# An mLSTM cell and a quick-GELU block on one core: another order in the second chunk

## The chip, the cores and the metric

The kernel runs on one core of a Trainium2 chip. The metric is the device time of one execution in microseconds (us), from six runs. One more execution was taken with the hardware profiler; its trace is what "the profile" means below. The engines are TensorE (PE, with its weight loads PEld), VectorE (DVE), ScalarE (ACT), GpSimd (POOL) and SyncE (SP), which issues most DMAs.

## The reference

An mLSTM cell runs over 768 steps for 4 batches of 8 heads (head dimension 40); its output is reshaped to 3072 tokens of 320 values and goes through a two-layer block with a quick GELU.

```python
for t in range(S):
    m_new = np.maximum(f_gate[:, :, t] + m, i_gate[:, :, t])
    f_stab = np.exp(f_gate[:, :, t] + m - m_new)
    i_stab = np.exp(i_gate[:, :, t] - m_new)
    m = m_new
    C = f_stab * C + i_stab * np.einsum('bhd,bhe->bhde', vt, kt)
    n = f_stab * n + i_stab * kt
    h_tilde = np.einsum('bhde,bhe->bhd', C, qt)
    denom = np.maximum(np.abs(np.einsum('bhd,bhd->bh', n, qt)), 1.0)
    y[:, :, t] = sigmoid(o_gate[:, :, t]) * h_tilde / denom

h = x @ w_in                      # 3072 x 320 @ 320 x 2048
out = (h * sigmoid(1.702 * h)) @ w_out   # 2048 x 320
```

## The kernel before

**Chunks.** The 768 steps are cut into six chunks of 128 (`w` = 0 to 5). Within a chunk the recurrence is written as attention: scores of queries and keys, times decay weights, times values, plus the queries times the state carried from the chunk before. "The second chunk" is `w = 1`, called chunk 1 here. `b` is one of the four batches.

**The main loop.** For each chunk `w` the kernel computes the up products (GELU hidden values of the chunk's 512 tokens), then the down products. The attention of chunk `w + 1` is put between the down blocks of chunk `w`. The order on every engine is the order in which the code issues the work: it is written out by hand, and each engine runs its queue in that order and waits where an input is not there.

**Chunk 0 is special.** Its up and down products are plain (`up`, `down`); from chunk 1 on they use sums of blocks that save products (`up_fast`, `down_fast`). The weights `w_in` and `w_out` come in as raw bits in twenty pieces; `fetch(n)` loads one, `convert(n)` turns it into 32-bit floats in two ACT and four DVE instructions. Pieces 10 to 19 are `w_out`; they are still being loaded and converted beside the down blocks of chunk 0.

**The 16 down blocks of chunk 0** (`blocks`, L796) go in the order: two blocks for each b, then one for each b, then one for each b. Block `i` = 12 to 15 ends the sum of batch `i - 12`: DVE copies it from PSUM to `o_sb` (L568) and ACT's queue stores it (L569). After the blocks whose numbers are in `stops` (L797) the next list of `attention(1)` (L645 to L649) is run. So the lists after blocks 10, 12 and 15 are: the first two seams; values of b = 2, 3 and the scalings; the last two seams, the new states and the carry.

**The parts of attention that matter here:**
- `values(w, ...)`: PE products of weights and values (`p_o`, L363) and of queries and state (`p_i`, L368). Then for each b a chain of seven DVE instructions (L383 to L393) makes `y`, reading the o gates `eo` in L391, and GpSimd copies 64 of its columns (L395).
- `scale_values` (L409) and `scale_state` (L415): GpSimd multiplies the values `v_st` and the `state` of one b in place by decay factors. They have to come after the products that read the old contents.
- `seam(w, b)`: three PE transposes of `y` (L402), the third of which needs the columns that GpSimd copied; ACT copies the result to `xT` (L403), the input of the up products.
- `new_states`: PE products of keys and scaled values (`p_c`, L428). `carry`: DVE adds them to the scaled state (L436); GpSimd sets the ones column of `v_st` (L439).
- `gates_out`: ACT's tanh of the o gates, in place (L343). It stands after the eight exponentials of `weights(1, 2)` (L335).

**The sums of `w_out`** (`weight_sums`, L583): sums 0 and 1 make `t1` and `t2` for the fast down products of chunk 1, which come some 35 us later. They need `w_out` converted in full.

**SP's queue.** All loads go through it in order. In the loop over chunk 0's up products, at `j == 4` (L776 to L781), come the o gates of chunk 1 (640 KB, one DMA), then piece 17 (two DMAs), then the values of chunk 1 (640 KB, one DMA of the same shape); pieces 18 and 19 and the keys follow. At block 10 the queue gets 32 small loads of chunk 2's keys and queries (`load_blocks(2)`, L117), which DVE transposes (L302) at the start of chunk 1's up products. The core's DMAs, loads and stores, share eight completion counters in turn, and a DMA is not issued before the one ahead of it on the same counter is complete.

Of the kernel before, what the change touches and what calls it, by code (L numbers as in the profile page):

```python
# [34 lines left out]
def kernel(  # L35
# [120 lines left out]
    def fetch(n):  # L156
        if 6 <= n < 10:
            bits[n] = gp.tile([128, 512, 2], U32, tag="g", name="bits")
        else:
            room = xs if n == 19 else big[:, n if n < 6 else (n - 10) % 6, :]  # L160
            bits[n] = room.bitcast(U32).rearrange("p (a two) -> p a two", two=2)
        for r, c, src in pieces[n][1]:
            dst = bits[n][r, c].rearrange("p a two -> p (a two)")
            if len(src.shape) == 3:
                dst = dst.rearrange("p (j m) -> p j m", j=src.shape[1])
            nc.sync.dma_start(out=dst, in_=src)
# [188 lines left out]
    def values(w, *bs, states=False):  # L355
        po, pi = {}, {}
        for b in bs:
            po[b] = ps_a.tile([L, H, D1], FP, tag="a", name="p_o")
            for p in range(NP):
                for i in range(2):  # L360
                    h = 2 * p + i
                    for t in HALVES:
                        T.matmul(po[b][t, h, :], wt[w, b][:, p, i, t], v_st[:, b * H + h, :], start=True, stop=True)  # L363
        for b in bs if w else ():
            pi[b] = ps_a.tile([L, H, D1], FP, tag="a", name="p_i")
            for p in range(NP):
                for t in HALVES:
                    T.matmul(pi[b][t, 2 * p:2 * p + 2, :].rearrange("p a b -> p (a b)"), qT[w, b][:, p, t],  # L368
                             state[:, b * NP + p].rearrange("p a b -> p (a b)"), start=True, stop=True)
        if states:  # L370
            for b in bs:
                scale_values(w, b)
        if states and w:

            new_states(w)
            for b in bs:
                scale_state(w, b)
        for b in bs:
            u = po[b]
            if w:  # L380
                u = work.tile([L, H, D1], FP, tag="u", name="u")
                g = cols[w][:, BH + b * H:BH + (b + 1) * H].unsqueeze(2).to_broadcast([L, H, D1])
                V.tensor_tensor(out=u, in0=pi[b], in1=g, op=OP.mult)  # L383
                V.tensor_tensor(out=u, in0=po[b], in1=u, op=OP.add)

            den = work.tile([L, H, 1], FP, tag="den", name="den")
            V.tensor_scalar(out=den, in0=u[:, :, D:D1], scalar1=-1.0, scalar2=1.0, op0=OP.mult, op1=OP.max)
            V.tensor_tensor(out=den, in0=u[:, :, D:D1], in1=den, op=OP.max)
            V.reciprocal(out=den, in_=den)
            z = eo[w][:, b * H:(b + 1) * H, :]  # L390
            V.scalar_tensor_tensor(out=z, in0=z, scalar=1.0, in1=u[:, :, 0:D], op0=OP.add, op1=OP.mult)  # L391
            y = ys[w, b] = work.tile([L, DM + 64], FP, tag="y", name="y")
            V.scalar_tensor_tensor(out=y[:, 0:DM].rearrange("p (h d) -> p h d", d=D), in0=z, scalar=0.5,  # L393
                                   in1=den.to_broadcast([L, H, D]), op0=OP.mult, op1=OP.mult)
            G.tensor_copy(out=y[:, DM:DM + 64], in_=y[:, DM - 64:DM])  # L395
# [185 lines left out]
    def weight_sums(n):  # L581
        out_, in0, in1 = ((t1, w01, w00), (t2, w11, t1), (t4, w10, t2), (w01, w11, w01))[n]
        V.tensor_tensor(out=out_, in0=in0, in1=in1, op=OP.subtract)  # L583
# [51 lines left out]
    def attention(w):  # L635
        if w > 1:

            return [[(columns, w)], [(weights, w, 0), (weights, w, 1)],
                    [(scores, w, 0), (hidden_sums, w - 1, 1, range(4), 3), (scores, w, 1), (weights, w, 2),
                     (weights, w, 3)],  # L640
                    [(values, w, 0), (values, w, 1), (scores, w, 2), (scores, w, 3)] +
                    [(scale, w, b) for b in (0, 1) if w + 1 < NW],
                    [(seam, w, 0), (seam, w, 1), (last_values, w)], [(carry, w)] if w + 1 < NW else [],
                    [(seam, w, 2)], [(seam, w, 3)]]
        return [[(columns, w)], [(weights, w, 0), (weights, w, 1)], [(scores, w, 0), (scores, w, 1)],  # L645
                [(weights, w, 2), (gates_out, w), (values, w, 0, 1), (scale, w, 0), (scale, w, 1)],
                [(weights, w, 3), (scores, w, 2), (scores, w, 3)], [(seam, w, 0), (seam, w, 1)],
                [(values, w, 2, 3), (scale, w, 2), (scale, w, 3)],
                [(seam, w, 2), (seam, w, 3), (new_states, w), (carry, w)]]  # L649

    def last_values(w):
        values(w, 2, 3, states=w + 1 < NW)
# [1 line left out]
    def run(calls):  # L654
        for f, *args in calls:
            f(*args)
# [98 lines left out]
    for w in range(NW):  # L755
        more = w + 1 < NW
        for j in range(NF // 2):
            if w == 0 and j == 0:
                for pair_ in range(2):
                    for i, g in enumerate(hidden_of(0, pair_)):  # L760
                        A.activation(out=g, in_=first[pair_][i], func=AF.Gelu_apprx_sigmoid)
                    if pair_ == 0:
                        weights_in(0)
            elif w == 0 and j % 2 == 0:
                weights_in(j // 2)
                up(j, j == 2)
            elif w and j % 4 == 0:
                up_fast(w, j, next_keys if more and j == 0 else None)
            if w == 0 and j == 0:
                load_blocks(1, 0)  # L770
                spread(1)
                load_blocks(1, 1)
            if w == 1 and j == 3:
                weight_sums(3)
            if more:
                if j == (0 if w else 4):  # L776
                    load(w + 1, "o")
                if j == 4:
                    if w == 0:
                        fetch(17)  # L780
                    load(w + 1, "v")  # L781
                    if w:
                        spread(w + 1)
                if j == (4 if w else 6):
                    load(w + 1, "k")
                if w and j == 3:
                    for b in range(2, 4):
                        transposes(w + 1, b)
            if w and j in (3, 7):
                hidden_sums(w, 0, (j // 4 * 2, j // 4 * 2 + 1), 1, 2)  # L790
                if j == 3:
                    hidden_sums(w, 0, (0, 1), 3, 4)
        side = attention(w + 1) if more else []
        if w == 0:

            blocks = [(lambda b=b, n=n: down(w, b, n)) for ns in ((0, 1), (2,), (3,)) for b in range(B) for n in ns]  # L796
            stops = (0, 1, 5, 6, 8, 10, 12, 15)  # L797
        else:
            blocks = down_fast(w, 0) + down_fast(w, 1)
            stops = (0, 1, 2, 4, 8, 10, 11, 12)  # L800
        for i, block in enumerate(blocks):
            if w == 0:
                weights_in(4 + i)
                if i == 0:
                    load_gates(2)
                if i == 2:
                    for b in range(B):
                        transposes(1, b, slice(0, 1))
                    first_sums((0, 1))
                    for b in range(B):  # L810
                        transposes(1, b, slice(1, 2))
                if i == 10:
                    load_blocks(2)
            elif w + 2 < NW and i == 0:
                load_gates(w + 2)
                load_blocks(w + 2)
            block()
            if i in stops and side:
                run(side.pop(0))
            if w == 1 and i == 1:  # L820
                weight_sums(2)
            if w:
                for at, c, *what in ((0, 0, (2, 3), 3), (1, 0, (2, 3), 4), (1, 1, range(4), 1),
                                     (5, 1, range(2), 2), (6, 1, range(2, 4), 2), (7, 1, range(4), 4)):
                    if i == at:
                        hidden_sums(w, c, *what)
                if i == 2 and not more:
                    hidden_sums(w, 1, range(4), 3)
            elif i in (12, 14):
                weight_sums(i // 2 - 6)  # L830


# [28 lines left out]
```

## Time and profile before

| | |
|---|---|
| six runs, median (lowest to highest) | 490.01 us (487.5 to 492.44) |
| the profiled execution, its own time | 490.47 us |
| its span in the trace | 488.8 us |
| granted TensorE clock | 1.0 of full speed |
| PE busy | 478.0 us (98%), 4076 instructions |
| PE weight loads busy | 395.8 us (81%) |
| DVE / ACT / POOL busy | 342.1 / 221.0 / 63.9 us |
| DMA | 44.87 MB, mean 92 GB/s, nearly all on SP's queue |

Times in a trace are counted from the span's start. PE's busy time is modelled from pipelined matmuls, so two that follow each other overlap a little in the list. A line of the timeline has the start, the length, the engine, the code line, the operation, the tiles written and read, the shape, how many instructions are merged into it and, in square brackets, how long the engine was idle before it and what released it. In the stage before 62 us the kernel loads and converts `w_in` and runs chunk 0's attention; from 66 to 115 us it runs the down blocks of chunk 0 with chunk 1's attention between them; from 119 us the up products of chunk 1 follow, and from there on the chunks repeat.

### The profile page before, as it was taken

The numbers are of one execution on the slowest core, as the hardware profiler recorded it, in microseconds if no ns is written. First come the engines' busy times: TensorE is split into PE (matmuls) and PEld (weight loads), VectorE is DVE, ScalarE is ACT, GpSimd is POOL, SyncE is SP. The second block draws the span as 40 slices with busy tenths as digits, with TensorE's granted clock in tenths as the row PEclk, the third lists the DMA queues.
The fourth block names the chain that finished last, engine by engine and source line by source line (L and its number), as shares of the span: only waits on it lengthen the run. The fifth ranks groups of instructions, "written<-read, shape, count | busy, mean of one in ns | idle before, by whom it ended". The sixth has DMA issues, their size and how long they took to land. (4 is left out here: it accounts for less than half of the span.)

```text
span 488.8 us, 10443 instructions
## 1 busy us (share of the span) xinstructions
PE 478.0 (98%) x4076; PEld 395.8 (81%) x4076; DVE 342.1 (70%) x855; ACT 221.0 (45%) x575; POOL 63.9 (13%) x103
## 2 busy tenths in 40 slices
PE   7999998999999999999999999999999999999997
PEld 4874455777788999777999877999977999977897
DVE  8788878659978965677776586686666786254831
ACT  6757764501468500476800474900364930255300
POOL 4030001314000240000322000232000120000000
PEclk9999999999999999999999999999999999999999
DMA  9999779964896200996100696300293000000000
GB/s 127 180 258 320 118 189 200 156 77 70 113 237 70 31 28 15 142 229 74 17 29 1 108 256 77 35 28 3 65 264 34 1 1 30 28 1 0 1 27 28
DMA packets 175953, 44.87 MB, mean 92 GB/s; under 512 B 164352, under 2 KB 169504, under 8 KB 175904
## 3 DMA queue, kind: packets, MB, share of 16 engines
q1 hardware_dynamic: 175328, 43.55, 48.4%
q8 instruction: 32, 0.52, 0.5%
q10 hardware_dynamic: 576, 0.66, 0.4%
q14 instruction: 17, 0.14, 0.1%
HBM read 40.17 MB, written 4.01 MB: 90 GB/s over the span
## 5 line engine op out<-in xcount | busy, mean ns | idle before, releaser
L613 PE MATMUL p_out<-w_out_sb,g 128*128 128x160 f32 x480 | 69.8, 301 | 0.0
L403 ACT COPY xT<-p_x 128x384 f32<-128x384 f32 x24 | 10.8, 481 | 128.1 <-PE p_x L402 112.0
L613 PEld LDWEIGHTS p_out<-w_out_sb,g 128*128 128x128 f32 x480 | 66.3, 190 | 0.9
L524 DVE TENSOR_TENSOR g<-p_u,g 128x256 f32<-128x256 f32 x80 | 33.7, 424 | 44.7 <-PE p_u L516 35.0
L521 ACT COPY g<-p_u 128x256 f32<-128x256 f32 x120 | 43.1, 377 | 41.3 <-PE p_u L516 37.1
L528 ACT ACTIVATE g<-g 128x256 f32<-128x256 f32 x120 | 42.4, 425 | 39.1 <-DVE g L524 39.1
L337 POOL TENSOR_SCALAR_AFFINE_SELECT wt<-wt 128x1024 f32<-128x1024 f32 x20 | 22.7, 1136 | 238.5 <-ACT wt L335 208.7
L618 DVE TENSOR_TENSOR o_sb<-o_sb,p_out 128x160 f32<-128x160 f32 x70 | 21.4, 317 | 42.2 <-PE p_out L613 41.8
L335 ACT ACTIVATE wt<-wt,cols 128x128 f32<-128x128 f32 x160 | 47.9, 393 | 0.0
L516 PE MATMUL p_u<-xT,w_in_sb 128*128 128x256 f32 x160 | 38.9, 382 | 0.0
L516 PE MATMUL p_u<-xs,big 128*128 128x256 f32 x160 | 37.9, 379 | 0.0
L544 PE MATMUL p_v<-xT,w_in_x 64*128 64x512 f32 x80 | 37.0, 602 | 0.0
L544 PE MATMUL p_u<-xT,w_in_x 64*128 64x512 f32 x80 | 37.0, 602 | 0.0
L353 DVE TENSOR_TENSOR wt<-p_s,wt 128x512 f32<-128x512 f32 x48 | 30.4, 682 | 8.8 <-POOL wt L337 6.7
L564 PE MATMUL p_out<-w_out_sb,g 128*128 128x320 f32 x128 | 36.1, 436 | 0.0
L613 PE MATMUL p_out<-t,big 128*128 128x160 f32 x240 | 35.5, 301 | 0.0
L516 PEld LDWEIGHTS p_u<-xT,w_in_sb 128*128 128x128 f32 x160 | 29.6, 190 | 5.4 <-DVE o_sb L618 1.5
L516 PEld LDWEIGHTS p_u<-xs,big 128*128 128x128 f32 x160 | 30.0, 190 | 4.6 <-ACT g L521 0.2
L613 PEld LDWEIGHTS p_out<-t,big 128*128 128x128 f32 x240 | 33.3, 190 | 0.2
L564 PEld LDWEIGHTS p_out<-w_out_sb,g 128*128 128x128 f32 x128 | 23.8, 190 | 9.9 <-issue 0.5
L524 DVE TENSOR_TENSOR g<-p_v,g 128x256 f32<-128x256 f32 x80 | 29.8, 415 | 0.0
L363 PEld LDWEIGHTS p_o<-v_st,wt 128*64 128x64 f32 x768 | 23.9, 138 | 5.7 <-DVE w_out_sb L237 3.3
(168 smaller groups left out, 851.5 us busy)
## 6 DMA issues: line engine op xcount, KB each, us to landing
wt<-m_row SPq DMA_DIRECT2D x20, 512.0 KB, 7.0
eo<-in_o_gate_dram SPq DMA_DIRECT2D x5, 640.0 KB, 5.6
v_st<-in_v_dram SPq DMA_DIRECT2D x5, 640.0 KB, 8.9
k_st<-in_k_dram SPq DMA_DIRECT2D x5, 640.0 KB, 11.4
out_dram<-o_sb SPq DMA_DIRECT2D x20, 160.0 KB, 1.8
big<-in_moe_w_in_dram SPq DMA_DIRECT2D x5, 512.0 KB, 6.7
k_bl<-in_k_dram SPq DMA_DIRECT2D x40, 64.0 KB, 2.9
q_bl<-in_q_dram SPq DMA_DIRECT2D x40, 64.0 KB, 2.8
```

The lines of the kernel that those rows point to most:

```text
L335: A.activation(out=x[:, h, :], in_=x[:, h, :], func=AF.Exp, scale=-1.0, bias=cols[w][:, b * H + h:b * H + h + 1])
L337: G.affine_select(out=x, in_=x, compare_op=OP.is_ge, fill=0.0, base=0, pattern=[[0, H], [1, L]], channel_multiplier=-1)
L353: V.tensor_tensor(out=wt[w, b][:, :, i, :], in0=pw[i], in1=wt[w, b][:, :, i, :], op=OP.mult)
L363: T.matmul(po[b][t, h, :], wt[w, b][:, p, i, t], v_st[:, b * H + h, :], start=True, stop=True)
L516: T.matmul(p[k][:, ts[t]], a[:, k // 2, k % 2 * 128:(k % 2 + 1) * 128], b, start=first, stop=True, skip_group_check=True)
L521: A.copy(out=g[k][i][:, ts[t]], in_=chain[k][:, ts[0]])
L524: V.tensor_tensor(out=g[k][i][:, ts[t]], in0=p[k][:, ts[pt]], in1=g[k][i][:, ts[t]], op=OP.add)
L528: A.activation(out=dst, in_=dst if src is None else src, func=AF.Gelu_apprx_sigmoid)
L544: T.matmul(p[k], w_in_x[r, k, :], x[r, 2, :], start=False, stop=True, skip_group_check=True)
L564: T.matmul(po, gs[w, f // 2][:, f % 2, b * L:(b + 1) * L], w_out_sb[:, f, :], start=(f == 0), stop=(f == NF - 1))
L613: T.matmul(po, a(f), b[:, f, :], start=(f == 0), stop=(f == NH - 1))
L618: V.tensor_tensor(out=dst, in0=x, in1=po, op=OP.add)
```

## The change

Four edits, all around chunk 1's attention:

- SP's queue: the values of chunk 1 are loaded where the o gates were, and the o gates after piece 17, where the values were.
- Values of b = 2, 3: GpSimd scales `v_st` and `state` before DVE's chains and GpSimd's copies of `y` are issued, not after them. The new states stay where they were, after block 15; `values` is reached through `last_values` with `states=True`, and a new branch for `w == 1` scales the state alone.
- The last two seams are run after block 14 and the new states and carry after block 15, so `stops` has nine entries and `attention(1)` nine lists.
- Weight sums 0 and 1 are both issued after block 11, ahead of DVE's copy of block 12, instead of after blocks 12 and 14.

```diff
         if states:
             for b in bs:
                 scale_values(w, b)
-        if states and w:
+        if states and w == 1:
+            for b in bs:
+                scale_state(w, b)
+        elif states and w:
 
             new_states(w)
             for b in bs:
...
-                [(values, w, 2, 3), (scale, w, 2), (scale, w, 3)],
-                [(seam, w, 2), (seam, w, 3), (new_states, w), (carry, w)]]
+                [(last_values, w)], [(seam, w, 2), (seam, w, 3)], [(new_states, w), (carry, w)]]
 
     def last_values(w):
         values(w, 2, 3, states=w + 1 < NW)
...
-                if j == (0 if w else 4):
+                if w and j == 0:
                     load(w + 1, "o")
                 if j == 4:
-                    if w == 0:
-                        fetch(17)
                     load(w + 1, "v")
                     if w:
                         spread(w + 1)
+                    else:
+                        fetch(17)
+                        load(1, "o")
...
-            stops = (0, 1, 5, 6, 8, 10, 12, 15)
+            stops = (0, 1, 5, 6, 8, 10, 12, 14, 15)
...
-            elif i in (12, 14):
-                weight_sums(i // 2 - 6)
+            elif i == 11:
+                weight_sums(0)
+                weight_sums(1)
```

On the engines' queues this moves: on PE the six transposes L402 ahead of the last four-step down block; on DVE two L583 ahead of the copy of block 12; on ACT the last store behind the two copies L403; on POOL two L409 and two L415 ahead of two copies L395; on SP the two 640 KB loads past the two DMAs of piece 17. No instruction is added or removed.

## The prediction

> **What bounds the kernel now.** I read the busy time by stage first, to see where TensorE (PE) is not busy; then PE's waits, to learn what ends its idle time; then the engines in order of time around the two waits.
>
> Busy time by stage (start:end, length, then busy us and instructions of each engine, clock, DMA share, GB/s):
>
> ```profile
> core 0: us, PE busy (x) PEld busy (x) DVE busy (x) ACT busy (x) POOL busy (x), PEclk, DMA share, GB/s
> ...
> 62.00:84.00 22.00, 21.76 (x103) 14.14 (x99) 18.52 (x29) 11.94 (x31) 2.72 (x2) 1.00 0.95 191
> 84.00:119.00 35.00, 31.34 (x373) 24.37 (x374) 24.19 (x51) 10.04 (x26) 12.28 (x14) 1.00 0.71 108
> 119.00:486.00 367.00, 366.38 (x3114) 321.12 (x3113) 248.53 (x653) 156.67 (x448) 38.95 (x61) 1.00 0.38 66
> ```
>
> After 119 us PE is idle 0.62 us of 367: it is the bound, at full granted clock, and whatever PE gains earlier should reach the end. In 84 to 119, where chunk 1's attention runs between the down products of chunk 0, it is idle 3.66 us. All waits of PE over 1 us in the whole span, beside one at the start:
>
> ```profile
> PE p_o L363 <- DMA v_st<-in_v_dram: 2.8, 1, 2.8
> PE p_c L428 <- POOL v_st L409: 1.1, 1, 1.1
> ```
>
> The two in order of time, on PE and on GpSimd (POOL):
>
> ```profile
> 86.57 2.07 PE L363 MATMUL p_o<-v_st,wt 128*64 128x41 f32 x64 [2.81 <-DMA v_st<-in_v_dram]
> ...
> 115.41 0.82 PE L402 MATMUL p_x<-ident,y 128*128 128x128 f32 x6
> 116.16 1.12 PE L428 MATMUL p_c<-v_st,k_st 128*40 128x41 f32 x48
> 118.37 0.51 PE L428 MATMUL p_c<-v_st,k_st 128*40 128x41 f32 x16 [1.09 <-POOL v_st L409]
> ```
>
> ```profile
> 113.56 1.37 POOL L395 COPY y<-y 128x64 f32<-128x64 f32 x1 [2.24 <-DVE y L393]
> 114.90 0.73 POOL L409 TENSOR_TENSOR v_st<-v_st,cols 128x328 f32<-128x328 f32 x1
> 115.60 2.03 POOL L415 TENSOR_TENSOR state<-state,cols 128x328 f32<-128x328 f32 x1
> 117.59 0.73 POOL L409 TENSOR_TENSOR v_st<-v_st,cols 128x328 f32<-128x328 f32 x1
> ```
>
> The last value scaling ends at 118.32 only because it stands behind two y copies that wait for DVE; its own inputs were there when p_o ended (107.76).
>
> **Part 1, v ahead of the o gates on SP's queue.** Both are one DMA of 640 KB and the same shape, so they trade places: v is issued at 74.51 instead of 79.47, the gates at 79.47. v's other inputs are early: the last reader and writer of v_st end by 43 us. The gates took 6.3 us to land from the early place, which puts v at 80.8; the slowest 640 KB load of this stretch (keys, 9.5 us) would put it at 84.0. PE is free for L363 at 83.76, and the weights' products (L353) end at 83.29. So the wait of 2.81 goes; at worst 0.25 stays.
>
> What is late in its place is the gates: 79.47 + 7.0 (v's landing there) = 86.5, against ACT's start of their tanh (L343) at 86.33. Tanh ends at 86.5 + 1.26 = 87.8; DVE's first use (L391, 90.87 before) comes at 88.06. Cost nothing, cover 0.3. Gone by 2.2 with the keys' row (9.5): then the PSUM bank that scores (1,2) need, freed by L384 at 89.96, comes at 92.2 against PE's 91.43, and the last w_out conversion (ends 100.57) at 102.8 against its product at about 102.5: up to 1.0 lost. Queued behind L343 on ACT are the conversion of piece 18 and weights (1,3), with over 2 us to their users. The pieces 17 to 19 and the keys stay where they were on SP: the DMA after the gates was held 3.84 us and that after v 4.41, and the kinds only swap.
>
> **Part 2, GpSimd's order.** After p_o ends (104.95 once shifted by 2.81) GpSimd does L409 twice, L415 twice, then the two y copies. v_st is scaled by 107, p_c comes at about 113.7: the 1.09 goes. The same order already runs in chunk 2, and its rows price what it does to DVE's chain beside it:
>
> ```profile
> 181.64 0.50 DVE L383 TENSOR_TENSOR u<-p_i,cols 128x328 f32<-128x328 f32 x1 [2.93 <-PE p_i L368]
> 182.17 0.50 DVE L384 TENSOR_TENSOR u<-p_o,u 128x328 f32<-128x328 f32 x1
> 182.71 0.53 DVE L387 TENSOR_SCALAR den<-u 128x8 f32<-128x8 f32 x1
> ```
>
> ```profile
> 181.79 1.42 POOL L415 TENSOR_TENSOR state<-state,cols 128x328 f32<-128x328 f32 x2
> 184.69 0.24 POOL L395 COPY y<-y 128x64 f32<-128x64 f32 x1 [1.48 <-DVE y L393]
> 187.24 0.24 POOL L395 COPY y<-y 128x64 f32<-128x64 f32 x1 [2.31 <-DVE y L393]
> ```
>
> L387 takes 0.53 instead of 0.17 there. From the chain's start to the end of the second copy it is 187.48 − 181.64 = 5.84; chunk 1's first chain, with no GpSimd work beside it, took 94.73 − 89.27 = 5.46.
>
> **Part 3, seams one block sooner.** PE does the same six transposes, before down block 15 (2.19 us) instead of after it. Shifted, the values end at 106.04; blocks 13 and 14 take 16/24 of 108.85..115.41 = 4.37, to 110.41; seam (1,2) 0.38, to 110.79. DVE's chain starts at 108.39 − 2.81 = 105.58, so by chunk 2's rows y of b = 3 is written at 111.11 and copied at 111.42. Seam (1,3) waits 0.32 for the first and 0.06 for the second: 0.38 lost. Bounds: 0 by the undisturbed chain (111.04), and 1.46 if both L415 (0.73 each) stopped DVE in full. I take 0.38, from the same order in chunk 2.
>
> [...]
>
> **Part 4, weight sums sooner.** Two L583 of 1.48 go ahead of output copy b = 0 on DVE. The last conversion ends at 103.38 − 2.81 = 100.57, the sums at 103.53, the copy (0.49) at 104.02; the chain's input comes at 105.58. Cost nothing, cover 1.56; beyond it each us delays the seam. They free DVE after the chain, where PE waited for neither.
>
> **Part 5, the stores and chunk 2's queries.** Stores b = 0 to 2 go ahead of ACT's two seam copies, store b = 3 behind them. In the listing of the built program every DMA shares one of eight completion counters and waits for the one before it there. Before, the sixth query load of chunk 2 waited for store 0 (108.30) and the thirteenth for store 1 (117.10); now the sixth waits for store 1, the eighth for store 2, the tenth for store 3. Block 15 ends at 111.55 + 2.19 = 113.74, its copy at 114.2, the store is issued (0.36) and lands 1.9 later: 116.4. Seven loads at 0.49 and 2.7 to land: the last at 116.4 + 6 × 0.49 + 2.7 = 122.0. DVE wants them (L302) at 126.28 − 3.52 = 122.76: cost nothing, but the cover falls from about 5 us to 0.7, plus 0.34 of DVE idle time in the adds that follow (L524).
>
> **Sum.** 2.81 + 1.09 − 0.38 = 3.52. The span 488.8 becomes 485.3, the profiled execution 490.47 becomes 486.95; the median shown is 0.46 lower, so 490.01 − 3.52 = **486.5**. The six runs spread over 4.9 us, so some jitter lies in the waits themselves. 0.5% is 2.45 us, about what a measurement here tells from no change.
>
> **Rivals.**
> [...]
> - *v is no sooner on chip (0.08).* The early issue gains nothing because the queue is full: 1.09 − 0.38 = 0.7, so 489.3. Against: the gates' own 6.3 from that slot.
> - *Slower: chunk 2's queries behind store 3 (0.08).* The seven last loads go at the slowest issue of this kind (1.35, a key load) and land in 3.1: 116.4 + 6 × 1.35 + 3.1 = 127.6, 4.8 after DVE wants them. Beyond the 0.34 of idle time every us is PE's, as the four L302 stand ahead of the adds that free PSUM. It decides from 3.52 + 0.34 = 3.9 late; the price here is 4.8 − 0.34 = 4.5 against the 3.52 gained: 491.0. For it: SP's loads did wait here (117.10). Against: their median issue is 0.49.
> - *Forecast (0.74)*, own range 485.2 to 487.8.
>
> **Range and chances.** 484.4 (no seam wait, and 1.7 us of jitter) to 489.4 takes in both smaller-gain rivals. The forecast falls beyond 0.5% 9 times in 10, the partly eaten case 3 in 10: faster 0.70. Within: 0.22. Slower: 0.08.
>
> **What would show it.** L363 at about 83.8 with no DMA ahead of it; tanh L343 within 0.5 us of 86.4; all four scalings of GpSimd ahead of its y copies and no wait at L428; a wait under 0.6 at the last seam; up products from about 115.3 instead of 118.81, and PE without a gap after. Wrong if v still ends a wait of PE over 1 us, if the last seam waits over 1.5, or if an L302 near 123 waits for a query load.

## The result, and the profile after

The changed kernel took 486.98 us in the median of 38 runs (486.63 to 490.11), the kernel before 489.03 in 78 (487.38 to 493.41). The ratio is 0.9949, 95% interval 0.9935 to 0.9962: faster by 0.5%, 2.05 us of the forecast's 3.52. The profiled executions differ by more: their spans are 488.8 and 485.1. Both facts matter below: the two traces agree with the forecast, the medians with a little over half of it. The profiled execution of the run with the swap only was disturbed (996 us) and is left out, so that run has times and no trace.

Lines of the changed kernel are three higher than before from L383 on (the transposes L402 are L405 there, L583 is L586). First its busy time by stage, cut 3.69 us sooner than before, just after the up products of chunk 1 start:

```profile
62.00:84.00 22.00, 22.00 (x118) 14.64 (x117) 18.57 (x30) 11.92 (x31) 2.72 (x2) 1.00 0.93 196
84.00:115.31 31.31, 31.21 (x365) 23.79 (x361) 24.39 (x51) 9.84 (x25) 10.09 (x15) 1.00 0.71 110
115.31:482.30 366.99, 366.42 (x3114) 322.20 (x3112) 248.70 (x654) 156.69 (x448) 38.79 (x59) 1.00 0.39 67
```

The middle stage has the same work in 31.3 us instead of 35.0, with 0.1 of PE idle instead of 3.7; in the long stage behind it, of the same length by these cuts, PE is as busy as before. PE and GpSimd in order of time:

```profile
83.51 2.07 PE L363 MATMUL p_o<-v_st,wt 128*64 128x41 f32 x64
...
110.20 1.28 PE L405 MATMUL p_x<-ident,y 128*128 128x128 f32 x6
111.31 2.32 PE L567 MATMUL p_out<-w_out_sb,g 128*128 128x320 f32 x8
113.56 1.43 PE L431 MATMUL p_c<-v_st,k_st 128*40 128x41 f32 x64
114.92 1.99 PE L519 MATMUL p_u<-xT,w_in_sb 128*128 128x256 f32 x8
```

```profile
104.78 0.74 POOL L412 TENSOR_TENSOR v_st<-v_st,cols 128x328 f32<-128x328 f32 x1 [0.19 <-PE p_o L363]
105.48 1.42 POOL L418 TENSOR_TENSOR state<-state,cols 128x328 f32<-128x328 f32 x2
108.38 0.24 POOL L398 COPY y<-y 128x64 f32<-128x64 f32 x1 [1.48 <-DVE y L396]
110.86 0.24 POOL L398 COPY y<-y 128x64 f32<-128x64 f32 x1 [2.24 <-DVE y L396]
```

L363 starts with no DMA ahead of it, p_c with no wait. The six seam transposes take 1.28 instead of 0.82: 0.46 of waiting for y of b = 3, copied at 111.10. Up products start at 114.92 instead of 118.81.

### The profile page after: what moved, and what is told of

The parts are those of the page before. It is cut to its first block, busy times and chain, and to the rows that moved or that the text cites. A ratio compares the mean times of both kernels' runs of the same rounds, so it can differ in the third digit from the quotient of the medians.

```text
span 485.1 us, 10445 instructions
## 1 busy us (share of the span) xinstructions
PE 478.5 (99%) x4076; PEld 396.9 (82%) x4076; DVE 342.8 (71%) x855; ACT 220.9 (46%) x575; POOL 61.6 (13%) x103
## 5 line engine op out<-in xcount | busy, mean ns | idle before, releaser
L527 DVE TENSOR_TENSOR g<-p_u,g 128x256 f32<-128x256 f32 x80 | 33.7, 424 | 44.6 <-PE p_u L519 35.0
L547 PE MATMUL p_u<-xT,w_in_x 64*128 64x512 f32 x80 | 37.0, 602 | 0.0
L547 PE MATMUL p_v<-xT,w_in_x 64*128 64x512 f32 x80 | 37.0, 602 | 0.0
L527 DVE TENSOR_TENSOR g<-p_v,g 128x256 f32<-128x256 f32 x80 | 29.8, 415 | 0.0
L547 PEld LDWEIGHTS p_v<-xT,w_in_x 64*128 64x128 f32 x80 | 14.2, 186 | 16.0 <-issue 16.0
```

Of the source, the lines that this page charges most:

```text
L527: V.tensor_tensor(out=g[k][i][:, ts[t]], in0=p[k][:, ts[pt]], in1=g[k][i][:, ts[t]], op=OP.add)
L547: T.matmul(p[k], w_in_x[r, k, :], x[r, 2, :], start=False, stop=True, skip_group_check=True)
```

## The experiments

**How steady the wait of 2.81 is: the swap alone, and all but the swap.** The first kernel is the kernel before with this edit; the second is the changed kernel with it taken back.

```diff
-                if j == (0 if w else 4):
+                if w and j == 0:
                     load(w + 1, "o")
                 if j == 4:
-                    if w == 0:
-                        fetch(17)
                     load(w + 1, "v")
...
+                    else:
+                        fetch(17)
+                        load(1, "o")
```

> Only the two 640 KB loads are swapped; GpSimd's order, seams and weight sums stay as before. Theory J (the wait for v differs from run to run, 0 to 5 us, about 1.3 in the median run, and the profile of before caught one of 2.8): no PE wait for v, p_c still waits about 1.1 for GpSimd; every run close together, 10%-90% spread under 1 us instead of 4.8; median 486.97 + 0.7 = 487.7, lowest about 487.3, as low as the best runs of before and no lower. Rival S (the wait is a steady 2.8 and the spread of before comes from the loads at the start): the spread of before stays, and lowest and median both fall by 2.8, to 484.6 and 486.2.

> The changed kernel with the two 640 KB loads put back; the other three parts stay. Theory J: the spread of before comes back (10%-90% some 4 to 5 us), lowest 486.7, median 489.03 - 0.7 = 488.3; in the profile PE waits for v by whatever that run drew, 0 to 5 us, and not for p_c. Rival S: spread as in before, lowest and median both 0.7 lower than before's if the other parts are worth that, and a PE wait for v of 2.8 within 0.3.

Swap only: median 487.51, and eleven runs between 487.28 and 487.83, where the runs of the kernel before beside it spread from 486.98 to 493.49 with a median of 488.47. Without the swap: median 487.84, spread again over 486.80 to 490.82, and in its profile a wait of another length:

```profile
84.47 2.07 PE L363 MATMUL p_o<-v_st,wt 128*64 128x41 f32 x64 [0.70 <-DMA v_st<-in_v_dram]
```

Rival S falls, and theory J holds in kind: the wait differs from execution to execution. That the best runs of the kernel before have next to none is read from their times, which are as low as those with the swap (486.98 and 487.28). Of J's sizes the median with the swap was nearly met (487.7), the one without it was not (488.3): beside the same runs of the kernel before the swap gains 1.0, and taking it back costs 0.9. Whether p_c still waited in the first kernel can't be read, as that run has no trace.

**The kernel before once more**, unchanged.

> The kernel before once more, for one more profile. Theory J: PE's wait for v is another number than 2.81, and the span is 488.8 less the difference (within 0.5): span = 486.0 + wait. Rival S: 2.8 within 0.3 again.

The span was 486.3, 2.5 less than in the first profile, with a wait 2.2 shorter. PE's waits, and SP's issue of the values (start and length first):

```profile
PE p_c L428 <- POOL v_st L409: 1.1, 1, 1.1
...
PE p_o L363 <- DMA v_st<-in_v_dram: 0.6, 1, 0.6
```

```profile
77.44 0.38 SPq L105 DMA_DIRECT2D v_st<-in_v_dram  x1
77.91 4.65 SPq L166 DMA_DIRECT2D big<-in_moe_w_out_dram  x3
```

v was issued at 77.44 here and at 79.47 in the first profile, while PE came to L363 within 0.3 us of the same time. SP issues 56 loads between 32 us and v. At the o gates, three DMAs ahead of v, the two traces are 1.8 us apart (72.75 here, 74.51 there), and at v 2.0. So the wait follows a drift of SP's loads against PE; what sets the drift isn't shown. p_c's 1.1 is the same in both.

**Why the upper runs are so far up: v one piece later still**, on the kernel before.

```diff
                 if j == 4:
...
-                    load(w + 1, "v")
                     if w:
+                        load(w + 1, "v")
                         spread(w + 1)
...
         for p in ahead:
             fetch(p)
+            if p == 18:
+                load(1, "v")
```

> The kernel before with chunk 1's values one piece later on SP's queue, behind piece 18. They land 1.5 to 4 us later, so PE waits 3 to 6 us at L363. Theory (the runs of before at 491 to 493 are those in which the wait was long enough for the clock to drop, as after the 2.8 us wait in the run with the gates behind the keys, where the granted clock was 0.5 for some 7 us): the granted clock falls below 1 in the products after L363, at least one of them takes over 1.3 times its length, and the time is 487.5 + the wait + 2 to 4, so 492 to 496. Rival (a wait costs its own length and no more): clock 1.0 there, 487.5 + the wait, 490.5 to 493.5.

The wait was 3.14, and it cost more than that. PE in order of time, then its stages (start:end, length, PE, PEld, DVE, ACT, POOL busy, granted clock, DMA share, GB/s):

```profile
86.84 3.64 PE L363 MATMUL p_o<-v_st,wt 128*64 128x41 f32 x64 [3.14 <-DMA v_st<-in_v_dram]
90.25 2.46 PE L368 MATMUL p_i<-state,qT 128*64 128x82 f32 x32
```

```profile
84.00:89.00 5.00, 2.16 (x41) 2.19 (x42) 2.16 (x2) 5.00 (x14) 1.09 (x1) 0.70 1.24 221
89.00:92.00 3.00, 3.00 (x54) 3.00 (x54) 0.34 (x1) 1.31 (x3) 0.00 (x0) 0.50 1.20 111
92.00:95.00 3.00, 3.00 (x20) 2.19 (x18) 2.79 (x9) 0.00 (x0) 0.24 (x1) 0.87 0.66 93
```

The granted clock fell to 0.5 and the two groups took 6.1 us instead of 3.4. This execution took 493.44 us; the ten runs lie between 489.66 and 494.61, median 491.28, under the theory's 492 and inside the rival's range, so here it is the clock and the lengths that decide, not the median.

The mean granted clock is known for every execution, without a trace too. Of these ten runs the four from 489.66 to 490.64 have 0.999 or 1.0, and the six from 491.23 up 0.993 to 0.997: not every execution with v this late had the slow clock. In 80 runs of the kernel before, taken beside these experiments, the 14 with 0.997 or less are exactly the 14 slowest, from 490.35 up; the other 66 end at 490.27. In 113 runs of kernels with the swap (those with the gates behind the keys left out) it was that low twice. So the upper runs of the kernel before are those with a slow clock, and it goes with the swap; of the 78 in the result, 25 lie above 490.5. That a long wait for v came before it in each of them isn't shown: the mean doesn't say where the clock fell.

**The seams back behind block 15**, everything else as changed.

```diff
-                [(last_values, w)], [(seam, w, 2), (seam, w, 3)], [(new_states, w), (carry, w)]]
+                [(last_values, w)], [(seam, w, 2), (seam, w, 3), (new_states, w), (carry, w)]]
...
-            stops = (0, 1, 5, 6, 8, 10, 12, 14, 15)
+            stops = (0, 1, 5, 6, 8, 10, 12, 15)
```

> The changed kernel with the last two seams back behind block 15, everything else as changed. If the seam's wait for y (0.46 of PE in the changed kernel) is a plain loss: no wait at the seam, up products start 0.4 sooner, median 486.97 - 0.4 = 486.6, span 484.7. Rival (the sooner seam pays for itself, because the seam copies on ACT or the stores are otherwise late for the up products): the same or up to 0.5 slower, with a wait of PE at the first p_v products or at p_u.

> The changed kernel with the seams behind block 15, again, beside new runs of the kernel before: median 486.55 within 0.2, 0.4 under the changed kernel's 486.98, ratio to before about 0.995 to 0.997.

Medians 486.55 (486.27 to 486.59) and 486.36: faster than the changed kernel by 0.4 to 0.6, and the six transposes take 0.82 with no wait in them. In this kernel the sooner seam is a plain loss. One execution of the second set took 489.37; its trace is at the end, in the section on the hardware.

**The weight sums back behind blocks 12 and 14**, first in the changed kernel, then with the seams late as well.

```diff
-            elif i == 11:
-                weight_sums(0)
-                weight_sums(1)
+            elif i in (12, 14):
+                weight_sums(i // 2 - 6)
```

> The changed kernel with weight sums 0 and 1 back behind blocks 12 and 14. If their place was worth nothing to PE (the prediction): median within 0.3 of 486.97; DVE is 3.0 later with the copy of block 15 and the carry some 0.5 later, up to 0.3 lost at the adds L527. Rival (DVE is the limit after the seam, so the sums' place is what makes the sooner order work): the carry or the transposes L302 are late by 1.5 or more and the up products wait, 1 to 2 us slower than the changed kernel.

> Only the swapped loads and GpSimd's order remain of the change: seams behind block 15, weight sums behind blocks 12 and 14. If the sums' place matters only because the sooner seam meets a y copy that GpSimd cannot make beside an L586 (1.37 instead of 0.24 in the run with late sums): no wait at the seam, which comes 2.2 later, and a median within 0.4 of the 486.55 of the run with the seams behind 15. Rival (the sums' place is worth 1.0 by itself, through DVE's carry and the work behind it): 487.5 or more, with PE waits in the up products.

In the changed kernel it costs 1.05 (488.03, 487.92 to 488.51), but not where either theory put it. DVE, GpSimd and PE at the seam:

```profile
110.59 1.48 DVE L586 TENSOR_TENSOR t<-w_out_sb 128x1280 f32<-128x1280 f32 x1
```

```profile
110.80 1.37 POOL L398 COPY y<-y 128x64 f32<-128x64 f32 x1 [2.23 <-DVE y L396]
```

```profile
112.23 0.33 PE L405 MATMUL p_x<-ident,y 128*128 128x128 f32 x1 [1.06 <-POOL y L398]
```

The copy takes 1.37 for 0.24 and ends at 112.17, L586 at 112.07, and the last transpose waits 1.06 for the copy. With the seams late as well, nothing waits at the seam, and my theory wanted 486.55; it was 487.46, so the rival won. Up products start at 114.66, as with late seams alone, but DVE comes to their adds (L527) at 125.90 instead of 124.99, and PE's weight loads for the products into p_u wait 1.0 for them. DVE in this run and in the run with late seams alone, then PE here:

```profile
125.90 1.42 DVE L527 TENSOR_TENSOR g<-p_u,g 128x256 f32<-128x256 f32 x4
```

```profile
124.99 1.42 DVE L527 TENSOR_TENSOR g<-p_u,g 128x256 f32<-128x256 f32 x4
```

```profile
125.29 1.12 PE L547 MATMUL p_v<-xT,w_in_x 64*128 64x512 f32 x2
126.38 0.69 PE L547 MATMUL p_u<-xT,w_in_x 64*128 64x512 f32 x1
...
130.00 1.99 PE L519 MATMUL p_u<-xs,w_in_sb 128*128 128x256 f32 x8
```

From the first of them to the next product it is 4.71 us; it is 3.90 with the sums sooner and was 3.63 in the kernel before:

```profile
129.37 0.69 PE L544 MATMUL p_v<-xT,w_in_x 64*128 64x512 f32 x1
...
133.00 1.99 PE L516 MATMUL p_u<-xs,w_in_sb 128*128 128x256 f32 x8
```

This run also holds only the swap and GpSimd's order, and is no faster than the swap alone (487.46 and 487.51).

**So GpSimd's order left out: the swap and the sooner sums only**, on the kernel before (the two edits shown above).

> The kernel before with the swapped loads and the two weight sums sooner; GpSimd's order and the seams stay as before. If the sums' late place was what made p_c wait (before, L583 held the y copy at 113.56 for 1.37 and an L415 for 2.03): GpSimd's chain of two copies and four scalings ends some 2.4 sooner without them, p_c does not wait, up products start where they do in the run with late seams, and the median is 486.4 as there; GpSimd's new order is then worth nothing by itself. Rival (GpSimd's order is needed as well): PE still waits at p_c, and the median stays at 487.0 or more.

Median 486.41 (486.28 to 486.63), as with GpSimd's order. Its GpSimd, still in the old order, and p_c:

```profile
110.67 0.24 POOL L395 COPY y<-y 128x64 f32<-128x64 f32 x1 [2.23 <-DVE y L393]
110.88 0.74 POOL L409 TENSOR_TENSOR v_st<-v_st,cols 128x328 f32<-128x328 f32 x1
111.57 0.74 POOL L415 TENSOR_TENSOR state<-state,cols 128x328 f32<-128x328 f32 x1
112.26 0.74 POOL L409 TENSOR_TENSOR v_st<-v_st,cols 128x328 f32<-128x328 f32 x1
```

```profile
113.28 1.43 PE L428 MATMUL p_c<-v_st,k_st 128*40 128x41 f32 x64
```

The copy takes 0.24 instead of 1.37 and the L415 0.74 instead of 2.03; the last scaling of v_st is done at 113.0, and p_c doesn't wait.

**One batch of transposes later.** The kernel with late seams, and for chunk 2 the transposes of b = 1 with those of b = 2, 3.

```diff
         transposes(w + 1, 0)
-        transposes(w + 1, 1)
+        if w > 1:
+            transposes(w + 1, 1)
...
-                    for b in range(2, 4):
+                    for b in range(1 if w == 1 else 2, 4):
```

> The kernel with the seams behind block 15, and DVE's two transposes of chunk 2, b = 1, moved from ahead of the first adds L527 to the other transposes of that chunk. If the 3.9 us that the L547 products take there instead of 3.63 are DVE's lateness at L527: they take 3.63 again, and the median falls by 0.3 to 486.1. Rival (something else spaces them, or DVE is short later): 486.4 as before, or the loss moves behind j = 3 and it is slower.

Median 486.10 (485.93 to 486.25), ratio to before 0.9952 [0.9938, 0.9966] on its own chip, where the kernel before took 488.84 in 11 runs; the swap and sums alone took 486.28 to 486.63 there, so this is the fastest of the versions, by 0.3. The products go in pairs again, 3.63 from the first to the next:

```profile
125.02 0.69 PE L547 MATMUL p_v<-xT,w_in_x 64*128 64x512 f32 x1
125.03 0.69 PE L547 MATMUL p_u<-xT,w_in_x 64*128 64x512 f32 x1
...
128.65 1.99 PE L519 MATMUL p_u<-xs,w_in_sb 128*128 128x256 f32 x8
```

**The o gates later**, to test their cover: behind piece 18, then behind the keys (the edit shown is the second).

```diff
                         fetch(17)
-                        load(1, "o")
...
                     load(w + 1, "k")
+                    if w == 0:
+                        load(1, "o")
```

> The changed kernel with chunk 1's o gates issued one piece later, behind piece 18. If the cover in the prediction is right (the tanh may end about 0.3 later than in the changed kernel at no cost to DVE, and DVE may be some 1.4 later before PE waits): the gates land at 88 to 90 instead of 86.1, L394 starts that much later, PE loses 0 to 2 us at scores (1,2), median 487.0 to 489. Rival (the gates have no cover, or far more than counted): every us of lateness is PE's, 2 to 4 us lost, or nothing is lost although L394 is over 2 us later.

> The changed kernel with chunk 1's o gates behind pieces 18 and 19 and the keys on SP's queue: issued at 84 to 87, landing at 91 to 95 instead of 86.1, so DVE's L394 comes at 92.5 to 96.5 instead of 87.8, 4.7 to 8.7 late. By the cover in the prediction (1.4 us of lateness free, then one for one at the second pair of score products and behind them): PE loses 3.3 to 7, median 490 to 494, and a PE wait at L351 or at a w_out product. Rival (most of the lateness is absorbed elsewhere): under 1.5 us lost.

Behind piece 18 (median 486.92) the gates landed at 85.3, no later than in the changed kernel: this tells nothing of the cover. Behind the keys it took 492.67. L394 came at 93.52, 5.7 late, and PE lost 6.4 by the start of the up products:

```profile
91.07 1.16 PE L351 MATMUL p_s<-qT,kT 40*128 40x128 f32 x16
95.01 2.60 PE L351 MATMUL p_s<-qT,kT 40*128 40x128 f32 x16 [2.77 <-DVE u L386]
97.54 6.62 PE L567 MATMUL p_out<-w_out_sb,g 128*128 128x320 f32 x16
```

```profile
95.00:97.50 2.50, 2.49 (x16) 2.27 (x16) 2.33 (x8) 2.50 (x9) 0.36 (x2) 0.50 0.65 57
97.50:100.00 2.50, 2.50 (x6) 1.68 (x6) 2.33 (x3) 0.58 (x2) 2.50 (x3) 0.50 0.79 105
```

Only 2.77 of it is waiting, so 2.9 of the lateness was free, not 1.4; the other 3.6 is the clock at 0.5, which makes 1.0 into 2.60 and 4.57 into 6.62. So the loss lies in the range expected, but over half of it by luck: the expectation had no slow clock in it.

## Why the prediction was right, and where it was not

In medians of separate sets of runs, built up edit by edit: before 489.03; the swap 487.51; with the sums 486.41; with GpSimd's order as well 486.36 to 486.55; with the sooner seams, the changed kernel, 486.98. So −1.5, −1.1, 0 and +0.5 us. The first step is the least certain: beside the swap's own runs of the kernel before (488.47) it is −1.0, 95% interval −0.1 to −2.4, and by taking the swap out of the changed kernel it is −0.9. Of the 1.5 us by which the gain of 2.05 falls short of 3.52, 1.0 is the starting time, whose median was 490.01 in six runs and 489.03 in 78; the time itself came 0.5 above the 486.5 forecast.

- *Part 1, "the wait of 2.81 goes"*: right in kind, and the term that was mis-sized. It is one draw of a wait that was 0.6, 0.7 and 2.8 in three traces without the swap. The median run gains 0.9 to 1.5 by the swap; by their times the runs over 490.5 gain 3 to 6 and the best ones nothing. The prediction had the sign of it in hand, a spread of 4.9 us in six runs, and still took the sum from the one trace. In the pair of traces its sum was good, 3.52 for 3.7, but by luck: from the second trace of the kernel before (486.3) to the changed kernel's (485.1) it is 1.2.
- *The gates*: tanh started at 86.18, where 86.5 was forecast, and cost nothing. That v is no sooner on chip is refuted: PE came to L363 at 83.51 and v was there. The cover of the PSUM bank was read at the wrong place. In the run with the gates behind the keys the first 16 score products, those of scores (1,2), ran at 91.07 with no wait; the second 16, those of scores (1,3), waited, and for L386 (L383 before), not for the L384 that the prediction names. So 2.9 us were free, not 1.4.
- *Part 2, "the 1.09 goes"*: it went, but this part was not what the time came from. That the sums were worth 1.1, the size of this term, is luck. The prediction blamed the place of the scalings behind the two y copies; the runs put it on L583, beside which a copy took 1.37 for 0.24 and an L415 2.03 for 0.74. GpSimd's order, with the swap alone beside it, leaves no wait at p_c (1.1 in the traces with the old order and late sums) and gives it back at L547 (4.71, with late seams alone 3.90), as DVE is 0.9 later there.
- *Part 3*: 0.38 forecast, 0.46 measured, from chunk 2's rows. DVE's L390 took 0.53 beside L418 here too.
- *GpSimd and DVE at once* was weighed at the wrong pair. Beside the scalings DVE lost 0.36, as the rows said: L386 and L387 kept their 0.50, and L390 took 0.53 for 0.17 and ended with L418, at 106.9. Where it decides is the y copy beside a weight sum: 1.37 for 0.24, and 1.06 of PE in the changed kernel with late sums. The prediction showed that very line, at 113.56, and priced only what the scalings cost DVE, with 1.46 as the bound; and it was not the only one in the trace, as the L415 of 2.03 lay beside the second L583. What the range calls the partly eaten case came neither by late gates, which took 6.4 to land where the keys' row had 9.5, nor by a scaling that stopped DVE in full.
- *Part 4, "cost nothing", "PE waited for neither"*: the step that failed. The sums' sooner place did cost nothing, but it was put at no gain, and it is worth 0.9 to 1.1 us, with the seams sooner through the y copy, with the seams late through the adds.
- *Part 5*: the last query load was issued at 119.5 (119.3 forecast), and the transposes at 122.74 (122.76) waited for none. Nothing was tried on it alone.
- *Not foreseen*: 0.26 in the L547 products of the changed kernel (3.89 for 3.63), which the later transposes win back.

## What to carry to other kernels

A wait for a load that drifts against the engine that needs it differs from trace to trace (0.6, 0.7 and 2.8 us here): take it from the spread of many runs, not from one trace, and expect the gain in the median (0.9 to 1.5 here) to differ from the gain in the slow tail (3 to 6). When a wait names a GpSimd instruction, look at the VectorE instruction beside it before reordering GpSimd: here a copy of 0.24 took 1.37 beside a sum of 1.48. A wait that is removed shows who was late behind it, as p_c's 1.1 came back as 1.08 at L547 (4.71 for 3.63); follow the next engine's instructions to the next place where TensorE needs them.

## What the runs showed of the hardware

The granted TensorE clock fell to 0.5 at idle gaps of 2.77 us (o gates behind the keys: mean clock 0.50 from 95 to 100 us, 0.66 from there to 102.5) and 3.14 us (v one piece later: 0.70 from 84 to 89 us, 0.50 to 92, 0.87 to 95), and cost 3.6 and 2.7 us on top of them; a gap of 2.81 in the first profile left it at 1.0. It was 0.5 at a still shorter gap, of 1.70, in the second set with late seams, near the start of its traced execution (PE, then two stages; the last three figures are granted clock, DMA share and GB/s):

```profile
18.52 1.08 PE L308 MATMUL p_t<-ident,q_bl 128*128 128x128 f32 x4 [1.70 <-DMA q_bl<-in_q_dram]
```

```profile
16.00:20.00 4.00, 2.11 (x11) 1.59 (x12) 3.69 (x10) 1.56 (x4) 0.61 (x2) 0.78 0.80 145
20.00:24.00 4.00, 4.00 (x42) 3.43 (x40) 0.21 (x2) 2.17 (x5) 0.00 (x0) 0.80 0.96 197
```

By an estimate from the two means, 0.78 and 0.80, the clock was 0.5 from about 18.2 to 21.6 us, and this execution took 489.37, 3.0 over the median of its set.

So in these traces gaps of 1.70, 2.77 and 3.14 us went with a clock of 0.5 and one of 2.81 with 1.0: the length of a gap alone doesn't tell, and what decides isn't shown.
